# Filling products for the token assignment, another place for the compaction products, and a second bank for the row transpositions

## The chip, the cores and the metric

The kernel is one program on one core of a Trainium2 chip. Its metric is the device time of one execution in microseconds (us); the median of three runs of the kernel before is 1051.88 us (1051.66 to 1055.12). A core has TensorE (PE in the profile, PEld for its weight loads), VectorE (DVE), ScalarE (ACT), GpSimd (POOL) and SyncE (SP, which here only issues DMAs). TensorE's clock has two levels, 2.4 and 1.2 GHz; the profile gives the granted clock of a stretch as a share of the upper one, so 1.00 is full and 0.50 is half.

## What is computed

```python
x = attention(q, k, v, g_q, g_k)            # 4 x 12 heads x 448 rows x 64, with RMS norms
x = moe(x, modality_id, w_gate, bias, w1, w2)   # 1792 tokens, 8 experts, argmax
# second layer of experts: every expert takes CAP = 1792 / 8 = 224 tokens
logits = x @ w_gate
for idx in np.argsort(-logits.flatten()):
    tok, e = idx // 8, idx % 8
    if assigned[tok] >= 0 or counts[e] >= cap:
        continue
    assigned[tok] = e; counts[e] += 1
for e in range(8):
    mask = assigned == e
    h = np.maximum(x[mask] @ w1[e], 0.0)     # 768 x 1024
    out[mask] = h @ w2[e]                    # 1024 x 768
```

The greedy assignment of the second layer ("token assignment") is what the change touches, together with the start of that layer's experts.

## The kernel before, in words

The program runs attention, then the first layer of experts (`moe1`), then the second (`moe2`). The assignment is the class `Assigner`. It works in phases: in each phase every free token bids for its best open expert, the rank of each bid among all bids is counted, and one expert becomes full; its 224 tokens are then known and it can be computed. Phase 0 works on all 1792 tokens (16 columns of 128). After it the free tokens are compacted to 7 columns (in the branch that this input takes), and phases 1 to 6 and a last one work on those.

The steps of a phase, with their lines: `bids` takes the maxima on DVE and transposes the bids on PE (L1673), ACT copies the rows out (L1675). `count` compares every bid with every row on DVE or ACT and counts by products on PE (L1718, in phase 0 also L1618 and L1590 of `one` and `late`), and transposes the counts (L1792). `settle` finds who was served (L1819 to L1824 on DVE), sums that over the partitions on PE (L1827), and names the full expert. `put` writes one-hot rows (L1901 on DVE) and gathers the tokens' numbers by products on PE (L1906). `compact` calls the function `before` (a prefix sum with two products, L1926) and moves the free tokens together by 16 float32 products (L1997, two records each) of a one-hot matrix that DVE writes (L1995).

The experts: `gather` fetches the rows of an expert's tokens in two halves of 112 by an indirect DMA on POOL (L2124). `turn` transposes a quarter of them (three PE transpositions, L2132), and ACT copies them out (L2136); from the third expert on DVE also takes the lower part (L2139). Experts 0 and 1 run in float32 (first layer L2147, second L2184, two records for each product); experts 2 to 7 split weights and rows into two parts (L2114 on ACT, L2116 on DVE; first layer L2155 and L2156, second L2187 to L2189). Weights come by DMAs from SP (L2105). The four `turn`s of expert 0 write four banks of PSUM; those of all later experts write one bank, `px0`.

The order of the instructions on each engine is written by a planner, `Pace`. A step of the assignment is a Python `yield` of an engine (p, v, s, g for PE, DVE, ACT, POOL), a cost and the time from which it is ready. `work` says the same for a step of the experts; before it issues its own instruction it lets the assignment issue all steps that are ready up to that time (plus `SLACK` = 0.3 on PE). A later ready time thus puts an instruction further back in its engine's queue, behind work of the experts. All engines run their queues in order. The four turns of expert 0 have the ready times 4.5, 4.5, 5.5 and 5.5 in the planner's clock, and its first layer's first products are ready once the rows of turns 0 and 2 are copied.

PSUM has eight banks. In `moe2` banks 0 and 1 serve the assignment, `pg2` and `px0` the first-layer products, `po3` the second-layer results; the pool that holds them follows on the pools of `moe1`.

Of the kernel before, what the change touches and what calls it, by code (L numbers as in the profile page):

```python
# [10 lines left out]
F32 = mybir.dt.float32  # L11
# [9 lines left out]
CP, NC = 112, 4  # L21
# [766 lines left out]
def moe1(tc, consts, rt, e0, slot0, xs, wt, qkv, x0, w1, w2, w_gate2, y, assigner):  # L788
# [8 lines left out]
    with ExitStack() as ctx:  # L797
# [493 lines left out]
        t = turned(t)  # L1291
# [27 lines left out]

        pace.along(final())  # L1320
# [144 lines left out]
class Assigner:  # L1465
# [11 lines left out]
    def __init__(self, tc, consts, pool, bank, y, l2):  # L1477
        nc = tc.nc
        self.tc, self.c, self.bank = tc, consts, bank
# [57 lines left out]

    def fill(self, c, ti):

        nc, lo, x = self.tc.nc, self.lo, self.x3[:, c, :]  # L1540
        nc.vector.tensor_single_scalar(lo, ti, 127, op=OP.bitwise_and)
        nc.vector.tensor_copy(out=x[:, 0:1], in_=lo)
        nc.vector.tensor_tensor(out=x[:, 1:2], in0=ti, in1=lo, op=OP.subtract)
        nc.vector.tensor_scalar(self.busy[:, c : c + 1], ti, float(N), 100.0, op0=OP.is_ge, op1=OP.mult)
# [27 lines left out]
    def late(self):  # L1572

        nc, L = self.tc.nc, NTP - 1
        one, all_ = self.g[1:3]
        self.cols = NTP

        def earlier():
            yield "v", 1.1, 0.0
            self.below(L, one)  # L1580

        t, to = yield from self.bids(L, L + 1, 0.0, earlier)
        ct, t1 = yield from self.one(L, one, t, to, True)
        yield from self.all_scalar(L, all_, L - ON_S[1], L)
        yield from self.all_vector(NT, self.g14, ON_S[0], NT)
        t = yield from self.all_vector(L, all_, 0, L - ON_S[1])
        for n, g in (NT, self.g14), (L, all_):
            t = yield "p", 0.5, t
            for j in range(n):
                nc.tensor.matmul(ct[:, n, :], lhsT=g[:, 128 * j : 128 * j + 128], rhs=self.ohb[:, j, :E], start=False, stop=j == n - 1, skip_group_check=True)  # L1590
        t = yield "v", 0.2, t
        nc.vector.tensor_tensor(out=self.w, in0=self.w, in1=ct, op=OP.add)
        yield from self.settle(0, 0.0)
# [8 lines left out]
    def one(self, L, one, to, t, done):  # L1602
# [12 lines left out]
        t = yield "p", 0.5, max(t1, to)  # L1615
        for c in range(L, -1, -1):

            nc.tensor.matmul(ct[:, c, :], lhsT=one[:, 128 * c : 128 * c + 128], rhs=self.ohb[:, L, :E], start=c == L, stop=c < NT or not done, skip_group_check=True)  # L1618
# [35 lines left out]
    def bids(self, c0, c1, t, meanwhile=None):  # L1654
# [13 lines left out]
        for i in range(c0, min(c1, self.cols), 4):  # L1668
            v = min(4, c1 - i, self.cols - i)
            pr = self.bank().rearrange("p (a b) -> p a b", a=4)[:, :v]  # L1670
            tr[i] = yield "p", 0.11 * v, max(tb, tr.get(i - 8, 0.0))
            for a in range(v):
                nc.tensor.transpose(pr[:, a, :], self.bid[:, i + a : i + a + 1].to_broadcast([128, 128]), c["ident"])  # L1673
            tr[i] = yield "s", 0.2 + 0.1 * v, tr[i]
            nc.scalar.activation(self.rows[:, i : i + v, :], pr, AF.Copy)  # L1675
# [13 lines left out]
    def count(self, t, to, logits=None, more=None):  # L1689
# [100 lines left out]
        t = yield "p", 0.11 * G, t  # L1790
        for a in range(G):
# [16 lines left out]
    def settle(self, n, t):  # L1808
# [17 lines left out]
        tn = yield "p", 0.1, t  # L1826
# [55 lines left out]
    def put(self, n, t, ones, eng):  # L1882
# [21 lines left out]
        t = yield "p", 0.05 * C, t  # L1904
# [11 lines left out]
    def before(self, free, t):  # L1916
# [6 lines left out]
        t = yield "p", 0.12, t  # L1923
# [37 lines left out]
    def compact(self, F, t):  # L1961
# [30 lines left out]
        for j in range(C):  # L1992
# [3 lines left out]
            tp[j] = yield "p", 0.15, max(to, td)  # L1996
# [12 lines left out]
def moe2(tc, consts, qkv, x0, asn, w1, w2, y, out):  # L2009
# [10 lines left out]
    with ExitStack() as ctx:  # L2020
# [6 lines left out]
        asn.bank, asn.counts = lambda: next(turns), lambda: next(turns)  # L2027
# [37 lines left out]
        def phases(few):  # L2065
            t = 0.0
            for n in range(1, E - 1):

                to = (FEW if n == 1 else 0) if few else MANY.get(n)
                if to:  # L2070
                    t = yield from asn.compact(to, t)
# [54 lines left out]
        def turn(n, g, px=px0):  # L2126

            h, i = divmod(g, 2)
            px = px[:, : 3 * CP].rearrange("p (k c) -> p k c", c=CP)
            t = work("p", 0.3, ready[h])  # L2130
            for k in range(3):
# [201 lines left out]
NAT = 2  # L2333
GATHER = 1.7
# [71 lines left out]
```

## Time and profile before

| | |
|---|---|
| median of 3 runs | 1051.88 us |
| profiled execution | 1050.93 us, span 1049.2 us, mean granted clock 0.966 |
| PE busy | 993.0 us (95%), 6232 instructions |
| PEld busy | 777.7 us (74%) |
| DVE / ACT / POOL busy | 576.2 / 508.9 / 276.3 us |
| HBM | 110.69 MB read, 17.44 MB written |

A busy time counts an instruction from its start to its modelled end, and products overlap, so the distance from one start to the next is the price of a product in a stream. The span is divided roughly so: attention to about 400 us, the first layer of experts to about 683 us, the token assignment's phase 0 to 704 us, then the eight experts of the second layer to about 1037 us, and the last stores.

### The profile page before, as it was taken

Reading aid. Unit: us, or ns where it says so; the run is one execution under the profiler, and the core shown is the slowest. Engines: PE = TensorE matmul, PEld = TensorE weight load, DVE = VectorE, ACT = ScalarE, POOL = GpSimd, SP = SyncE. Lnnn points to the kernel's source line nnn. Section 1 sums busy time; section 2 is a strip of 40 time slices with the busy share of each in tenths; the row PEclk is TensorE's granted clock in tenths of the full one; section 3 lists DMA queues with packets and bytes.
Section 4 is the critical chain, followed back from the end, with each engine's and each line's share of the span. In section 5 each row is a group of like instructions: output and inputs, shape, how many; then the busy total and the mean of one; then the engine's idle time right before and its main releaser. Section 6 shows DMA issues by size and latency. Waiting matters only on the chain. (4 is left out here: it accounts for less than half of the span.)

```text
span 1049.2 us, 19190 instructions
## 1 busy us (share of the span) xinstructions
PE 993.0 (95%) x6232; PEld 777.7 (74%) x6232; DVE 576.2 (55%) x1543; ACT 508.9 (48%) x1127; POOL 276.3 (26%) x379
## 2 busy tenths in 40 slices
PE   8999999999998999999999998949999999999995
PEld 6666666666655688888888997738666789889995
DVE  5677877877875541111312121585878777666650
ACT  3777777777685422122441222641214466556640
POOL 5665555555522310100061111010010111011000
PEclk7799999999999999999999999967999999999998
DMA  7566666666365144628621011015932575585620
GB/s 160 124 148 155 145 150 159 145 151 162 86 183 188 32 173 147 219 93 290 229 71 33 32 62 37 17 48 231 327 113 91 190 243 174 201 278 149 217 78 29
DMA packets 80898, 151.05 MB, mean 144 GB/s; under 512 B 14254, under 2 KB 53422, under 8 KB 80752
## 3 DMA queue, kind: packets, MB, share of 16 engines
q1 hardware_dynamic: 75552, 126.06, 40.6%
q0 software_dynamic: 5200, 23.33, 7.2%
q8 instruction: 56, 0.92, 0.3%
q14 instruction: 90, 0.74, 0.2%
HBM read 110.69 MB, written 17.44 MB: 122 GB/s over the span
## 5 line engine op out<-in xcount | busy, mean ns | idle before, releaser
L224 DVE TENSOR_REDUCE nm<-sp 112x1 f32<-112x448 f32 x192 | 117.2, 620 | 69.3 <-PE sp L219 49.1
L230 ACT ACTIVATE e<-sp,nm 112x448 f32<-112x448 f32 x192 | 122.3, 638 | 29.4 <-DVE nm L224 25.5
L238 PE MATMUL tp<-ident,e 112*112 112x112 f32 x768 | 113.0, 271 | 0.0
L238 PEld LDWEIGHTS tp<-ident,e 112*112 112x112 f32 x768 | 82.5, 136 | 25.8 <-issue 16.4
L244 ACT ACTIVATE et<-tp 112x448 f32<-112x448 f32 x144 | 78.7, 546 | 39.6 <-PE tp L238 38.4
L2155 PE MATMUL bank<-xx,w1h 128*128 128x448 f32 x288 | 93.7, 381 | 0.0
L219 PE MATMUL sp<-bt,at 128*112 128x448 f32 x188 | 84.9, 452 | 1.0 <-DMA bt<-cut 0.4
L251 PE MATMUL op<-et,qkv 112*64 112x448 f32 x384 | 82.8, 552 | 0.0
L2195 POOL DMA_INDIRECT out_dram<-x,ids x16 | 17.0, 1064 | 247.4 <-ACT x L2194 157.5
L909 PE MATMUL pg<-w1h,xh 128*128 128x512 f32 x180 | 75.5, 419 | 6.5 <-PEq L1237 5.0
L932 PE MATMUL po<-w2h,hh 128*128 128x384 f32 x224 | 79.0, 353 | 0.1
L2156 PE MATMUL bank<-xx,w1l 128*128 128x224 f32 x288 | 77.2, 268 | 0.0
L933 PE MATMUL po<-w2l,hh 128*128 128x384 f32 x224 | 75.3, 336 | 0.1
L934 PE MATMUL po<-w2h,hl 128*128 128x384 f32 x224 | 75.3, 336 | 0.0
L911 PE MATMUL pg<-w1h,xl 128*128 128x512 f32 x180 | 71.6, 398 | 0.0
L910 PE MATMUL pg<-w1l,xh 128*128 128x512 f32 x180 | 71.5, 397 | 0.0
L2187 PE MATMUL bank<-w2h,hh 128*112 128x384 f32 x192 | 66.2, 345 | 0.0
L2189 PE MATMUL bank<-w2h,hl 128*112 128x384 f32 x192 | 64.6, 337 | 0.0
L2188 PE MATMUL bank<-w2l,hh 128*112 128x384 f32 x192 | 64.6, 337 | 0.0
L999 DVE COPY yt<-py 128x384 f32<-128x384 f32 x26 | 13.3, 552 | 90.6 <-PE py L998 90.6
L923 DVE TENSOR_TENSOR hl<-ph,hh 128x512 fp32r<-128x512 f32 x28 | 19.4, 691 | 79.4 <-ACT hh L922 47.4
L2116 DVE TENSOR_TENSOR w2l<-qkv,w2h 128x768 fp32r<-128x768 f32 x48 | 44.6, 957 | 26.9 <-ACT w2h L2114 20.8
(454 smaller groups left out, 2216.1 us busy)
## 6 DMA issues: line engine op xcount, KB each, us to landing
qkv<-in_moe_w_dram SPq DMA_DIRECT2D x88, 384.0 KB
qkv<-in_moe_w_dram SPq DMA_DIRECT2D x36, 512.0 KB
raw<-in_moe_w_dram SPq DMA_DIRECT2D x24, 512.0 KB
bt<-cut SPq DMA_DIRECT2D x96, 112.0 KB
at<-cut SPq DMA_DIRECT2D x96, 112.0 KB
w1s<-in_moe_w_dram SPq DMA_DIRECT2D x12, 512.0 KB
w2s<-in_moe_w_dram SPq DMA_DIRECT2D x16, 384.0 KB
qkv<-in_v_dram SPq DMA_DIRECT2D x12, 448.0 KB
```

What stands on the lines that cost most here:

```text
L219: nc.tensor.matmul(sp, lhsT=at[:, h, cs], rhs=bt[:, h, :], start=h == 0, stop=h == 1)
L224: nc.vector.tensor_reduce(out=st["nm"][:, n : n + 1], in_=sp, axis=AX.X, op=OP.max, negate=True)
L230: nc.scalar.activation(e, st.pop(("s", n)), AF.Exp, bias=st["nm"][:, n : n + 1], accum_out=st["sm"][:, n : n + 1])
L238: nc.tensor.transpose(tp[:, kc, :], e[:, kc * CP : (kc + 1) * CP], ident[:CP, :CP])
L244: nc.scalar.activation(dst, tp, AF.Copy)
L251: nc.tensor.matmul(st["op"][h * D : (h + 1) * D, :], lhsT=raws[i // 2][:, 2, 2 * (i % 2) + h, kc * D : (kc + 1) * D], rhs=st["et"][:, h, k ...
L909: nc.tensor.matmul(pg, lhsT=xh[:, k, :], rhs=w1h[:, k, fs], start=k == 0, stop=False)
L932: nc.tensor.matmul(po[n], lhsT=hh[:, k, :], rhs=w2h[:, kk, cs], start=kk == 0, stop=False)
L933: nc.tensor.matmul(po[n], lhsT=hh[:, k, :], rhs=w2l[:, kk, cs], start=False, stop=False)
L934: nc.tensor.matmul(po[n], lhsT=hl[:, k, :], rhs=w2h[:, kk, cs], start=False, stop=kk == KF - 1)
L2155: nc.tensor.matmul(pg, lhsT=h[:, k, fs], rhs=xx[:, k].rearrange("p a c -> p (a c)"), start=k == 0, stop=False)
L2156: nc.tensor.matmul(pg[:, :CAP], lhsT=l[:, k, fs], rhs=xh[:, k, :], start=False, stop=k == KD - 1)
```

## The change

A method `busy_pe(n)` issues n products of 512 columns of a matrix of ones into a bank that nothing reads (`spare`: a bank of `moe1` towards its end, `px0` at the start of `moe2`). It is called in front of ten kinds of PE steps of the assignment and once, with 16, in front of expert 0's first transposition; after that `spare` is `None` and no more are issued. The ready times of L1827 and L1906 in all phases but phase 0, and of L1926 where `spare` is `None`, become 0.4 later in the planner's clock; those of the compaction products (L1997) become 2.0 later. `turn` uses `px0` and `pg2[0]` in turn for all experts but the first.

```diff
--- before.py
+++ after.py
@@ -1317,6 +1317,7 @@
             yield "v", 0.1, t
             nc.vector.tensor_copy(out=asn.m[:, NTP - 1, :], in_=pl)
 
+        asn.spare = ps1.tile([128, 512], F32, name="pg")
         pace.along(final())
         pace.rest()
         send(yr, ti)
@@ -1476,7 +1477,7 @@
 
     def __init__(self, tc, consts, pool, bank, y, l2):
         nc = tc.nc
-        self.tc, self.c, self.bank = tc, consts, bank
+        self.tc, self.c, self.bank, self.spare = tc, consts, bank, None
         tile = lambda name, shape, dt=F32: pool.tile(shape, dt, name=name)
 
         self.m, self.l2 = l2[:, :, :E], l2
@@ -1535,6 +1536,14 @@
         self.mn, self.busyn, self.x3n = tile("mn", [128, most + 1, E]), tile("busyn", [128, most + 1]), tile("x3n", [128, most, 3])
         nc.gpsimd.memset(self.x3n, 1.0)
 
+    def busy_pe(self, n):
+
+        if self.spare is None:
+            return
+        ones = self.c["ones"]
+        for _ in range(n):
+            self.tc.nc.tensor.matmul(self.spare.rearrange("p (a b) -> p a b", a=4), lhsT=ones, rhs=ones.unsqueeze(1).to_broadcast([128, 4, 128]), start=True, stop=True)
+
     def fill(self, c, ti):
 
         nc, lo, x = self.tc.nc, self.lo, self.x3[:, c, :]
@@ -1586,6 +1595,7 @@
         t = yield from self.all_vector(L, all_, 0, L - ON_S[1])
         for n, g in (NT, self.g14), (L, all_):
             t = yield "p", 0.5, t
+            self.busy_pe(1 if n == NT else 4)
             for j in range(n):
                 nc.tensor.matmul(ct[:, n, :], lhsT=g[:, 128 * j : 128 * j + 128], rhs=self.ohb[:, j, :E], start=False, stop=j == n - 1, skip_group_check=True)
         t = yield "v", 0.2, t
@@ -1613,6 +1623,7 @@
         nc.vector.scalar_tensor_tensor(one[:, lo : lo + 128], flat[:, lo : lo + 128], self.bid[:, L : L + 1], self.tri, op0=OP.subtract, op1=OP.is_lt)
         ct = self.bank()[:, : (L + 1) * E].rearrange("p (c e) -> p c e", e=E)
         t = yield "p", 0.5, max(t1, to)
+        self.busy_pe(5 if done else 1)
         for c in range(L, -1, -1):
 
             nc.tensor.matmul(ct[:, c, :], lhsT=one[:, 128 * c : 128 * c + 128], rhs=self.ohb[:, L, :E], start=c == L, stop=c < NT or not done, skip_group_check=True)
@@ -1669,6 +1680,7 @@
             v = min(4, c1 - i, self.cols - i)
             pr = self.bank().rearrange("p (a b) -> p a b", a=4)[:, :v]
             tr[i] = yield "p", 0.11 * v, max(tb, tr.get(i - 8, 0.0))
+            self.busy_pe(6)
             for a in range(v):
                 nc.tensor.transpose(pr[:, a, :], self.bid[:, i + a : i + a + 1].to_broadcast([128, 128]), c["ident"])
             tr[i] = yield "s", 0.2 + 0.1 * v, tr[i]
@@ -1788,6 +1800,7 @@
         nc.scalar.activation(pcs[:r, x : 128 * G], pc[:r, x : 128 * G], AF.Copy)
         ct = self.bank().rearrange("p (a q w) -> p a q w", a=4, q=4)[:, :G]
         t = yield "p", 0.11 * G, t
+        self.busy_pe(3)
         for a in range(G):
             nc.tensor.transpose(ct[:, a].rearrange("p q w -> p (q w)"), pcs[:, 128 * a : 128 * a + 128], c["ident"])
         if more:
@@ -1823,7 +1836,8 @@
         with nc.allow_low_precision("counts up to 14"):
             nc.vector.tensor_reduce(out=self.ns, in_=u.rearrange("p c e -> p e c"), axis=AX.X, op=OP.add)
         pn = self.bank()[:, :E]
-        tn = yield "p", 0.1, t
+        tn = yield "p", 0.1, t + (LATER if n else 0.0)
+        self.busy_pe(6)
         nc.tensor.matmul(pn, lhsT=c["ones"], rhs=self.ns, start=True, stop=True)
 
         t = yield "v", unit, tu
@@ -1901,7 +1915,8 @@
             nc.vector.tensor_scalar(self.a[:, i, :], self.i112, k[:, i : i + 1], None, op0=OP.is_equal)
         t = max(t, tv)
         pi = self.bank()[:CP, : 4 * E]
-        t = yield "p", 0.05 * C, t
+        t = yield "p", 0.05 * C, t + (LATER if n else 0.0)
+        self.busy_pe(14)
         for j in range(C):
             nc.tensor.matmul(pi, lhsT=self.a[:, j, :], rhs=self.place[:, j, :], start=j == 0, stop=j == C - 1)
         table = self.table.rearrange("p e h w -> p e (h w)")
@@ -1920,7 +1935,8 @@
         f = self.fb[:, :P]
         t = yield "v", 0.1, t
         nc.vector.tensor_scalar(f, self.busy[:, :P], 50.0, None, op0=OP.is_lt)
-        t = yield "p", 0.12, t
+        t = yield "p", 0.12, t + (0.0 if self.spare else LATER)
+        self.busy_pe(8)
         pf = self.bank()[:, : 2 * P].rearrange("p (i c) -> p i c", i=2)
         for i, m in enumerate(("ut", "ones")):
             nc.tensor.matmul(pf[:, i, :], lhsT=c[m], rhs=f, start=True, stop=True)
@@ -1958,7 +1974,7 @@
         self.halves()
         yield from self.put(n, t, iter(range(self.cols)), nc.vector)
 
-    def compact(self, F, t):
+    def compact(self, n, F, t):
 
         nc = self.tc.nc
         C = self.cols
@@ -1993,7 +2009,7 @@
             o = self.g[j // have % 2].bitcast(F32)[:, 128 * (j % have) : 128 * (j % have) + 128]
             to = yield "v", 0.2, max(t, tp.get(j - 2 * have, 0.0))
             nc.vector.tensor_scalar(o, self.i128, b[:, j : j + 1], None, op0=OP.is_equal)
-            tp[j] = yield "p", 0.15, max(to, td)
+            tp[j] = yield "p", 0.15, max(to, td) + (BEHIND if n == 1 else LATER)
             nc.tensor.matmul(px, lhsT=o, rhs=data[:, j].rearrange("p n x -> p (n x)"), start=j == 0, stop=j == C - 1)
         px = px.rearrange("p (n x) -> p n x", n=F)
         t = yield "v", 0.5, tp[C - 1]
@@ -2024,7 +2040,7 @@
         bank = [ps.tile([128, 512], F32, name=f"bank{i}") for i in range(8)]
         pg2, po3, px0 = bank[2:4], bank[4:7], bank[7]
         turns = cycle(bank[:2])
-        asn.bank, asn.counts = lambda: next(turns), lambda: next(turns)
+        asn.bank, asn.counts, asn.spare = lambda: next(turns), lambda: next(turns), px0
 
         raws = [t[:, FF * i : FF * i + FF] for t in qkv for i in range(3)]
         xx = p2.tile([128, KD, 2, CAP], F32R, name="xx")
@@ -2068,7 +2084,7 @@
 
                 to = (FEW if n == 1 else 0) if few else MANY.get(n)
                 if to:
-                    t = yield from asn.compact(to, t)
+                    t = yield from asn.compact(n, to, t)
                 t = yield from asn.phase(n, t)
             yield from asn.last(E - 1, t)
 
@@ -2123,11 +2139,14 @@
             fetched.append((n, h))
             nc.gpsimd.indirect_dma_start(out=xgs[h], out_offset=None, in_=y, in_offset=IndirectOffsetOnAxis(ap=asn.ids[:, n, h : h + 1], axis=0))
 
-        def turn(n, g, px=px0):
+        def turn(n, g, px=None):
 
             h, i = divmod(g, 2)
-            px = px[:, : 3 * CP].rearrange("p (k c) -> p k c", c=CP)
+            px = (px or (px0, pg2[0])[g % 2])[:, : 3 * CP].rearrange("p (k c) -> p k c", c=CP)
             t = work("p", 0.3, ready[h])
+            if n == g == 0:
+                asn.busy_pe(16)
+                asn.spare = None
             for k in range(3):
                 nc.tensor.transpose(px[:, k, :], xgs[h][:, (3 * i + k) * 128 : (3 * i + k + 1) * 128], ident[:CP, :CP])
             yield
@@ -2331,6 +2350,8 @@
 EARLY = 0.3
 NHR = 5
 NAT = 2
+LATER = 0.4
+BEHIND = 2.0
 GATHER = 1.7
 FIRST = 1
 NHR = 5
```

## Rows read from the trace of the kernel before

**Rows 1.** Busy time by stretch: start:end, length, each engine's busy us, granted clock, DMA share, GB/s.
```profile
690.00:695.00 5.00, 2.12 (x46) 1.57 (x46) 4.63 (x11) 4.95 (x14) 0.00 (x0) 0.52 0.00 0
...
710.00:715.00 5.00, 5.00 (x28) 5.00 (x27) 2.04 (x13) 1.35 (x3) 0.00 (x0) 0.50 1.03 404
```

**Rows 2.** Timeline of PE, 705 to 722 us: start, us, line, out<-in, count, idle before.
```profile
708.20 0.82 PE L2132 MATMUL bank<-ident,xg 112*128 112x112 f32 x3 [3.71 <-DMA xg<-y,ids]
...
713.76 3.98 PE L1997 MATMUL bank<-rows,g 128*128 128x77 f32 x18
717.54 1.78 PE L2147 MATMUL bank<-xtt,w1s 128*128 128x224 f32 x4
...
721.17 2.44 PE L2147 MATMUL bank<-xtt,w1s 128*128 128x224 f32 x12
```

**Rows 3.** Timeline of PE, 656 to 661 us, after a pause.
```profile
656.56 0.80 PE L909 MATMUL pg<-w1h,xh 128*128 128x512 f32 x1 [4.98 <-PEq L1237]
...
658.01 0.63 PE L909 MATMUL pg<-w1h,xh 128*128 128x512 f32 x1
658.43 0.63 PE L910 MATMUL pg<-w1l,xh 128*128 128x512 f32 x1
...
660.10 0.39 PE L909 MATMUL pg<-w1h,xh 128*128 128x512 f32 x1
660.33 0.39 PE L910 MATMUL pg<-w1l,xh 128*128 128x512 f32 x1
```

**Rows 4.** Timeline of PE, 691 to 705 us: steps of phase 0 that wait.
```profile
691.58 0.47 PE L1673 MATMUL bank<-ident,bid 128*128 128x128 f32 x1 [1.05 <-DVE w L1805]
...
700.64 1.90 PE L1906 MATMUL bank<-place,g 128*112 128x32 bf16 x16 [3.32 <-POOL place L1893]
704.29 0.17 PE L1926 MATMUL bank<-fb,ut 128*128 128x16 bf16 x1 [1.75 <-DVE fb L1922]
```

**Rows 5.** Timeline of all engines, 692 to 706 us: work beside those steps.
```profile
692.46 0.35 DVE L1613 SCALAR_TENSOR_TENSOR g<-rows,bid,tri 128x128 bf16<-128x128 f32 x1 [0.27 <-ACT rows L1675]
692.73 2.35 DVE L1628 TENSOR_TENSOR g<-rows,bid 128x512 bf16<-128x512 f32 x2
...
699.26 2.95 DVE L1901 TENSOR_SCALAR g<-i,k 128x112 bf16<-128x112 bf16 x13
...
705.52 0.94 POOL L2124 DMA_INDIRECT xg<-y,ids  x1 [0.30 <-DVE t L1934]
```

**Rows 6.** DMA issues, 706 to 707.5 us: count, median us from issue to landing.
```profile
xg<-y,ids POOLq DMA_INDIRECT x1, 6.0
```

**Rows 7.** Chain that ended last, 744 to 860 us: start, us, what.
```profile
744.99 0.83 PE bank L2184 x2
...
747.09 0.29 PE bank L2132 x3
...
855.00 5.36 DMA qkv<-in_moe_w_dram
```

**Rows 8.** Timeline of PE, 843 to 848 us: around two transpositions of expert 2.
```profile
843.69 0.33 PE L2189 MATMUL bank<-w2h,hl 128*112 128x384 f32 x1
844.58 0.51 PE L2132 MATMUL bank<-ident,xg 112*128 112x112 f32 x3 [0.56 <-DVE xx L2139]
...
846.84 0.33 PE L2189 MATMUL bank<-w2h,hl 128*112 128x384 f32 x1
847.27 0.51 PE L2132 MATMUL bank<-ident,xg 112*128 112x112 f32 x3
```

**Rows 9.** Timeline of PE, 800 to 1000 us: products that stood idle before their start.
```profile
803.62 0.51 PE L2132 MATMUL bank<-ident,xg 112*128 112x112 f32 x3 [0.53 <-DVE xx L2139]
...
862.52 0.17 PE L1827 MATMUL bank<-ns,ones 128*128 128x8 bf16 x1 [0.69 <-DVE ns L1824]
...
935.54 0.22 PE L1906 MATMUL bank<-place,g 128*112 128x32 bf16 x1 [2.29 <-DVE g L1901]
...
989.22 0.51 PE L2132 MATMUL bank<-ident,xg 112*128 112x112 f32 x3 [0.57 <-DVE xx L2139]
```

## The prediction

> **What bounds the kernel now.** I read the granted clock by stretch first, then PE's timeline where it is low, then the chain that ended last, then the products that stood idle. Four things are to be seen.
>
> From 690 to 720 us the clock is at half. Between 690 and 695 PE is busy for 2.12 of 5.00 us; between 710 and 715 it is busy all the time and still has 0.50 [rows 1]. That second stretch holds row transpositions and compaction products L1997, and these do not bring the clock back: 18 records of L1997 take 3.78 us, 0.21 each [rows 2]. Only expert 0's first layer brings it back: its first four records stand about 0.39 apart, those from 721.17 on 0.20 [rows 2].
>
> Up to 708.20 the assignment itself is the bound, a chain of short steps on DVE, ACT and PE, and PE stands idle in it: 1.05 us before L1673, 3.32 before L1906, 1.75 before L1926, 3.71 before the first row transposition [rows 2, 4].
>
> From 708.20 to the layers' end PE is the bound, with work in its queue all the time.
>
> From expert 2 on PE halts at two kinds of places: at row transpositions, which wait until DVE has read the one bank of the group before, and at assignment steps at an expert's start, which wait for DVE [rows 8, 9].
>
> **The fillers.** The trace of before has no bfloat16 product of 512 columns over the whole array. The nearest rows are L909 and L910, 512 columns: 0.42 us apart at half clock, 0.23 at full [rows 3]. I take 0.23 where the clock holds and keep 0.42 for the range; less than nothing is excluded for the product itself, because its result is not read and its gain is the clock. In phase 0's tail there are 3 in front of L1792, 1 and 5 in front of L1618, 6 of L1673, 1 and 4 of L1590, 6 of L1827, 14 of L1906, 8 of L1926, 16 of the first row transposition.
>
> At full clock 14 take 3.2 us of 3.32 idle, 8 take 1.84 of 1.75, 16 take 3.7 of 3.71 [rows 2, 4]: covered to a tenth each. L1906 has more cover: its 16 products follow the one-hots of L1901, which DVE writes for 2.95 us from 699.26 on [rows 5]. If that cover is gone (fillers at half clock) each overruns, which is a rival below.
>
> The six in front of L1673 are the exception. L1673 waited for DVE's L1805, the last reader of the earlier pool's banks [rows 4], though its own input, the bids, needs no such step. The fillers write a bank of the same new pool. If they wait for the same release, they start at 691.58 and L1673 is 6 x 0.23 = 1.4 late; if their bank is free they start when PE ran dry, 691.58 - 1.05 = 690.53, and end at 691.9, 0.35 late. I take 1.2, near the first, because the row shows a release by a reader of the old pool. Queued behind L1673 is ACT's copy L1675, and for that waits L1613 on DVE [rows 5]; L1628 follows it in DVE's queue, L1590 waits for L1628, and the rest of phase 0 hangs on that. So 1.2 us are lost on the path, up to the gathers and weight issues.
>
> **Expert 0's layer ahead of the compaction.** By the ready times, L1997 (about 4.8 in the planner's clock, now 2.0 more) no longer stands between the four turns (4.5 and 5.5). The first layer is ready when turns 0 and 2 are copied, 7.6 by my working of the planner's costs (four transposition groups of 0.3 up to 6.1, then copies of 0.45). By then six of the sixteen compaction products (12 records) are ready and go ahead of it, and ten (20 records) go among its first products. PE thus waits for the second half of the rows: issued at 705.52, 6.0 to landing [rows 5, 6], 711.5, and with the 1.2 from above 712.7. Two transposition groups at full clock, 0.29 each [rows 7], and 12 records at 0.105 (half of 0.21) end at 714.5. That is the start of L2147, in place of 717.54 [rows 2].
>
> From that start to L2184 before were 744.99 - 717.54 = 27.45 us [rows 2, 7], of which the 3.63 us up to 721.17 ran at half clock: at full 1.8 less. With 20 records of L1997 (2.1) among them, L2184 starts at 714.5 + 25.65 + 2.1 = 742.25. Gain 2.7 us, the 1.2 already off. The compaction ends some microseconds later against the layer; its customer, expert 1's tokens, has over 20 us of slack, since expert 1 begins only when expert 0's second layer is done.
>
> **Two banks.** At an expert's second group the last product starts at 843.69 and the next could go 0.175 later, but the transposition starts at 844.58: 0.71 lost; at the third 847.27 - 846.84 - 0.175 = 0.26 [rows 8]; the fourth I take as the third. That is 1.2 us for each of experts 2 to 6, and 0.5 for expert 1, where only the second group waits [rows 9]. With two banks a group waits for the reader of the group before the last, which is done by then. It counts only where PE bounds: in experts 1, 5 and 6 (of six such waits, one in each expert, rows 9 show the first and the last). In experts 2 to 4 PE waits anyway at the next expert's first assignment step (three waits, 0.69 the first and 2.29 the last [rows 9]) for DVE, which waits for weights whose DMA took 5.36 us [rows 7]; there the saved time turns into a longer wait. Sum 0.5 + 2 x 1.2 = 2.9. A new wait is possible: the next layer's first product writes `pg2[0]`, which the fourth group now holds until it is copied; it is copied ten microseconds before.
>
> **The later ready times.** 0.4 in the planner's clock lets one or two pairs of first-layer products (0.32 each in the code) go ahead of L1827, L1926 or L1906. At the three waits at expert starts that is 0.3 to 0.6 each: I take 1.2 in all. It is no loss unless a step moves to a place where DVE is later still: bounds 0 and 3.7 (all three waits gone) and, for a shifted step, one more wait of 2.3 to the bad.
>
> **Sum.** 2.7 + 2.9 + 1.2 = 6.8 us. The profiled execution took 1050.93 (span 1049.2 and 1.73 around it), 0.95 below the median of 1051.88; it gives 1044.1, and the median 1045.1.
>
> **Rivals.** *The clock falls again before the first layer.* Between the last filler and L2147 lie two transposition groups, an idle wait of 2 to 3 us for the second half of the rows, two more groups and 12 compaction records. For it: the dense stretch of the same instructions at 0.50 [rows 1], and the half clock after a pause of 4.98 us [rows 3]. Against: this stretch is shorter than the 30 us at half clock of before. The Trainium skill ("TensorE: Matmul & The Clock Gate", Part 4: PE-mode transpose) says that transposes do not count as PE activity in the way products do; the trace agrees, with 0.50 in a stretch with PE fully busy. Time: two groups at 0.56 (708.20 to the next start) and 12 records at 0.21 put L2147 at 716.35, 3.6 us at half lose 1.8, and L2184 starts at 716.35 + 25.65 + 2.1 + 1.8 = 745.9, 0.9 late. With 2.9 and 1.2: gain 3.2, 1048.7.
>
> *The banks bring nothing.* DVE and the weights bound all experts from 2 on. Against: in experts 5 and 6 no assignment step waits at the start. Then 2.7 + 0.5 + 0.6 = 3.8: 1048.1.
>
> *Slower: the fillers are the new wait.* If the clock has fallen by 691 us and the fillers do not bring it back, each costs 0.42: six 2.5 late, 14 take 5.9 of 3.32 (2.6 late), 8 take 3.4 of 1.75 (1.6), 16 take 6.7 of 3.71 (3.0): 9.7 late in place of 1.2, so 8.5 worse than my sum, 1053.6, and with the first layer at half clock 1056. It decides from the point where fillers before L1906 still run at half. Against: dense 512-column products brought the clock back between 656.56 and 660.10 [rows 3], and at half clock the fillers are dense.
>
> **Chances.** My forecast 0.48, the falling clock 0.25, no gain from the banks 0.15, fillers as the wait 0.08; 0.04 for steps of the assignment that land badly. About 0.5% (5.3 us, the time 1046.6) is what a measurement of this kernel can tell. The forecast's own range is 1041.5 to 1047.5, so most of it and a fifth of the second case are faster: 0.50; same 0.42; slower 0.08. Eight in ten lie between 1041 and 1050.
>
> **What would show it.** Right: granted clock near 1.00 from 695 on; fillers 0.2 apart; L2147 starting near 714 at 0.2 apart; no PE idle before L2132 from expert 1 on. Wrong: fillers 0.42 apart in front of L1906; a first row transposition after 710; the first records of L2147 at 0.39; longer waits before L1827 or L1906 by what the banks saved.

## The result and the profile after

| | before | after |
|---|---|---|
| median of 6 runs | 1055.73 us (1051.66 to 1057.85) | 1041.05 us (1037.0 to 1053.93) |
| profiled execution | 1050.93, span 1049.2 | 1044.16, span 1042.4 |
| mean granted clock | 0.966 | 0.974 |
| PE busy | 993.0 (x6232) | 1000.5 (x6296) |
| DVE / ACT busy | 576.2 / 508.9 | 575.6 / 505.8 |

The ratio of after to before is 0.9888 (0.9852 to 0.9924), some 11.8 us of the forecast's 1051.88. The six runs of before include the three of the forecast; the slowest run of after, 1053.93, fell in a slower state and is left out of the ratio. The two profiled executions are 6.8 us apart, but the part of the program that no edit touches took 3.1 us longer in the profile of after. So all marks below are counted from a fixed point, the last product with the router's weights (L1033): 685.20 us before, 688.28 after. Over the fourteen profiles of this case that point lies between 682.3 and 691.3, with no edit ahead of it; the runs do not show why it varies. Counted from it, the experts' last product ends at 351.3 before and at 341.7 after: 9.7 us.

The stretches of low clock, after (start:end, length, busy us of PE, PEld, DVE, ACT, POOL, then the granted clock, DMA share, GB/s):

```profile
692.00:693.00 1.00, 1.00 (x5) 0.54 (x3) 1.00 (x2) 1.00 (x5) 0.00 (x0) 0.50 0.00 0
...
695.00:700.00 5.00, 4.47 (x47) 2.34 (x46) 3.60 (x9) 3.45 (x7) 0.00 (x0) 1.00 0.00 0
...
705.00:710.00 5.00, 4.39 (x26) 2.50 (x25) 3.61 (x20) 0.28 (x1) 1.39 (x2) 0.86 0.33 107
710.00:715.00 5.00, 5.00 (x24) 2.26 (x23) 3.71 (x14) 0.00 (x0) 1.12 (x3) 0.80 0.74 187
715.00:720.00 5.00, 4.23 (x38) 4.02 (x35) 3.10 (x18) 1.58 (x4) 0.00 (x0) 1.00 1.03 378
```

The clock still falls twice, near 692 and near 709, for some 3 us each, and not for 30 us as before [rows 1]. Where expert 0's layer begins it is full. PE's timeline there (L1545 are the fillers; L2151, L2013 and L2166 are the row transpositions, compaction products and first layer that were L2132, L1997 and L2147):

```profile
691.47 1.42 PE L1545 MATMUL pg<-ones 128*128 128x512 bf16 x3
...
695.52 1.46 PE L1545 MATMUL bank<-ones 128*128 128x512 bf16 x6 [0.96 <-DVE w L1818]
696.81 0.27 PE L1685 MATMUL bank<-ident,bid 128*128 128x128 f32 x1
...
702.10 3.18 PE L1545 MATMUL bank<-ones 128*128 128x512 bf16 x14
705.57 1.86 PE L1921 MATMUL bank<-place,g 128*112 128x32 bf16 x16 [0.28 <-POOL place L1907]
707.75 2.76 PE L1545 MATMUL bank<-ones 128*128 128x512 bf16 x8 [0.32 <-issue]
...
710.41 4.41 PE L1545 MATMUL bank<-ones 128*128 128x512 bf16 x16
714.65 0.74 PE L2151 MATMUL bank<-ident,xg 112*128 112x112 f32 x6
716.16 0.79 PE L2151 MATMUL bank<-ident,xg 112*128 112x112 f32 x6 [0.77 <-DMA xg<-y,ids]
716.79 1.47 PE L2013 MATMUL bank<-rows,g 128*128 128x77 f32 x12
718.10 0.59 PE L2166 MATMUL bank<-xtt,w1s 128*128 128x224 f32 x2
```

The six fillers before L1685 (L1673 before) wait for the same reader of the old pool as that instruction did [rows 4], start with its release at 695.52 and put it 1.29 us back. The 14 before L1921 fit: they take 3.18 us, and L1921 then still waits 0.28 for POOL. The 8 ran partly at half clock (2.76 us for the group) and held the prefix sum back: it starts at 710.31, 22.0 from the mark, 19.1 before. But the first layer of expert 0 starts when the second half of its rows has come (716.16) and 12 compaction records are through, at 718.10: 29.8 from the mark, 32.3 before [rows 2], with products 0.2 apart.

Who PE waited for from expert 0's layer to the end, after (us in total, times, longest); below it the waits of before at the starts of experts 3 to 5:

```profile
PE bank L2174 <- DVE hr L2182: 2.9, 4, 1.3
PE bank L1730 <- DVE g L1765: 1.1, 1, 1.1
PE bank L1921 <- DVE g L1915: 0.9, 2, 0.5
PE bank L2151 <- DMA xg<-y,ids: 0.2, 1, 0.2
```

```profile
PE bank L1906 <- DVE g L1901: 2.3, 1, 2.3
PE bank L1926 <- DVE fb L1922: 0.7, 1, 0.7
PE bank L1827 <- DVE ns L1824: 0.7, 1, 0.7
```

No transposition waits for DVE any more, and the three waits of before at an expert's start are gone, the one of 2.29 us among them [rows 9]. Other steps of the assignment wait in their place, for 2.0 us in all (L1730 and L1921), and PE waits in the first layers of experts 3 to 6 (L2174) for DVE's part of the relu, which frees its banks.

### The profile page after: what moved, and what is told of

Read it like the earlier page. It is cut to its first block, busy times and chain, and to the rows that moved or that the text cites. A ratio compares the mean times of both kernels' runs of the same rounds, so it can differ in the third digit from the quotient of the medians.

```text
span 1042.4 us, 19307 instructions
## 1 busy us (share of the span) xinstructions
PE 1000.5 (96%) x6296; PEld 779.8 (75%) x6296; DVE 575.6 (55%) x1543; ACT 505.8 (49%) x1127; POOL 275.2 (26%) x379
## 5 line engine op out<-in xcount | busy, mean ns | idle before, releaser
L238 PEld LDWEIGHTS tp<-ident,e 112*112 112x112 f32 x768 | 82.9, 137 | 25.9 <-issue 16.3
L2174 PE MATMUL bank<-xx,w1h 128*128 128x448 f32 x288 | 93.2, 379 | 2.9 <-DVE hr L2182 2.9
L2174 PEld LDWEIGHTS bank<-xx,w1h 128*128 128x128 f32 x288 | 54.1, 188 | 9.5 <-DVE hr L2182 4.0
```

Of the source, the lines that this page charges most:

```text
L238: nc.tensor.transpose(tp[:, kc, :], e[:, kc * CP : (kc + 1) * CP], ident[:CP, :CP])
L2174: nc.tensor.matmul(pg, lhsT=h[:, k, fs], rhs=xx[:, k].rearrange("p a c -> p (a c)"), start=k == 0, stop=False)
```

## The experiments

Each kernel was profiled once and timed beside the kernel before. The marks are in us from the last L1033, read from PE's timelines: the first row transposition of expert 0 (T), the start of its first and of its second layer, the start of the second layers of experts 2 and 5, and the end of the last expert. "Ratio" is of time to that of before, with its interval.

| kernel | T | first layer 0 | second layer 0 | second layer 2 | second layer 5 | end | ratio |
|---|---|---|---|---|---|---|---|
| before | 23.0 | 32.3 | 59.7 | 155.2 | 265.4 | 351.3 | |
| after | 26.4 | 29.8 | 55.7 | 149.4 | 257.5 | 341.7 | 0.9888 (0.9852 to 0.9924) |
| after, again | 25.8 | 29.7 | 55.6 | 149.0 | 256.5 | 340.5 | 0.9897 (0.9856 to 0.9937) |
| no fillers | 22.9 | 29.9 | 58.6 | 152.0 | 259.4 | 342.8 | 0.991 (0.988 to 0.9941) |
| one bank | 25.7 | 29.5 | 55.4 | 148.8 | 255.9 | 342.0 | 0.9902 (0.9865 to 0.9939) |
| 16 fillers alone | 25.0 | 28.8 | 54.6 | 148.0 | 255.3 | 339.1 | 0.9855 (0.9825 to 0.9886) |
| LATER = 0 | 25.7 | 29.3 | 55.8 | 149.8 | 257.7 | 341.8 | 0.9898 (0.9864 to 0.9932) |
| BEHIND = 0 | 25.8 | 31.5 | 56.3 | 148.8 | 254.8 | 338.0 | 0.9875 (0.9836 to 0.9914) |
| only the banks | 22.8 | 32.3 | 59.7 | 154.4 | 272.6 | 356.6 | 1.0035 (1.0008 to 1.0062) |
| only the fillers | 26.4 | 31.7 | 57.4 | 152.9 | 264.7 | 350.7 | 0.9989 (0.9953 to 1.0025) |
| only LATER | 23.1 | 32.6 | 59.8 | 152.3 | 259.0 | 345.0 | 0.9926 (0.9893 to 0.996) |
| LATER and banks | 23.1 | 32.3 | 58.8 | 151.3 | 259.8 | 343.1 | 0.9907 (0.9874 to 0.9939) |
| 16 fillers, BEHIND = 0 | 25.0 | 29.7 | 54.5 | 147.0 | 254.4 | 338.7 | 0.9832 (0.9792 to 0.9872) |
| the same, LATER = 0.8 | 24.4 | 29.6 | 54.0 | 146.3 | 250.6 | 335.4 | 0.9822 (0.9778 to 0.9865) |

The intervals of the times overlap for most of these; the marks separate them better, since they leave out the part ahead. Two profiles of the changed kernel differ by 1.2 us at the end, so an end that differs by less says nothing.

**The changed kernel again.** No edit.

> The changed kernel itself, beside the other three on one chip. All marks are counted from the last product with the router's weights (L1033, 685.20 us in the profile of before, 688.28 in that of after), because the part ahead of it differs by 3.1 us between those two profiles without any edit there. Theory: the change is worth what lies behind that mark, 9.7 us in the two profiles (last product of the experts at 351.3 before, 341.7 after): time 0.987 to 0.993 of before; first layer of expert 0 starts near 30, its second layer near 56. Rival: the mark itself moves by an effect of the change, then the stretch ahead of it is longer than before's again by about 3 us.

The gain is behind the mark again, 10.8 us, and the marks are as in the first profile. The theory holds. The rival's longer stretch ahead came (691.3), but kernels with some of the edits have their mark anywhere from 682.3 to 690.0, so the runs do not tie it to the change.

**Without fillers.**

```diff
     def busy_pe(self, n):
-        if self.spare is None:
-            return
+        return
```

> The changed kernel without any filling product. Theory (the fillers' gain is the clock at expert 0's first layer): the clock is at half from about 5 us after the mark (the last router product) on; nothing delays the gathers, so the second half of the rows lands at 26.3, two transposition groups (0.56 each) and 12 compaction records (0.21 each) follow, the first layer starts at 30.0 and runs at half for about 3 us or more; its second layer starts at 58 to 59 (55.7 with fillers, 59.7 in the kernel before), and the kernel is 2 to 3 us slower than the changed one. Rival (the order alone does it: the layer comes before the compaction and wakes the clock itself early): second layer at 55.5 to 56.5, time within 1 us of the changed kernel.

Busy time by stretch and PE's timeline without fillers:

```profile
710.00:715.00 5.00, 3.12 (x16) 3.12 (x16) 2.51 (x15) 1.35 (x3) 0.00 (x0) 0.50 1.02 402
715.00:720.00 5.00, 5.00 (x21) 4.85 (x21) 0.00 (x0) 0.00 (x0) 0.00 (x0) 0.50 1.02 410
720.00:725.00 5.00, 5.00 (x30) 4.82 (x30) 2.15 (x12) 0.91 (x2) 0.00 (x0) 0.85 0.85 341
```

```profile
713.06 2.71 PE L2012 MATMUL bank<-rows,g 128*128 128x77 f32 x12
715.56 1.04 PE L2165 MATMUL bank<-xtt,w1s 128*128 128x224 f32 x2
...
721.56 0.59 PE L2165 MATMUL bank<-xtt,w1s 128*128 128x224 f32 x2
```

The first layer starts at 29.9, as early as with fillers, because it waits for the rows in both; but it runs at half clock until about 721, and the second layer starts at 58.6: 3.0 late, as the theory said. At the end 1.1 and 2.3 us are left of it, against the two profiles of the changed kernel.

**One bank.**

```diff
-            px = (px or (px0, pg2[0])[g % 2])[:, : 3 * CP]...
+            px = (px or px0)[:, : 3 * CP]...
```

> The changed kernel with the row transpositions of experts 1 to 7 in the one bank of before. Theory: the waits for the reader of the one bank come back in all of experts 1 to 6; they cost 0.5 to 1.1 us at expert 1 and about 1.3 each at experts 5 and 6, while in experts 2 to 4 the loss is regained at the next wait for DVE: 3 to 4 us slower than the changed kernel, with the experts' end at 345 to 346 after the mark. Rival (DVE and the weights bound every expert from 2 on): end within 1 us of the changed kernel's 341.7.

PE's waits with one bank, same columns as above:

```profile
PE bank L2151 <- DVE xx L2158: 3.0, 5, 0.7
PE bank L1921 <- DVE g L1915: 0.2, 1, 0.2
```

The waits for the one bank's reader come back in five experts (not in expert 1), and the waits of the first layers for DVE go. Up to the second layer of expert 5 one bank is 0.6 to 1.6 ahead of the two profiles with two banks, at the end 0.3 and 1.5 behind. So the theory's size (3 to 4) is not there, and the rival's end (within 1 us of 341.7) is; a table below shows where the gain went.

**Only the 16 fillers ahead of the first transposition.** All the other calls of `busy_pe` get 0, as these two:

```diff
-            self.busy_pe(1 if n == NT else 4)
+            self.busy_pe(0)
...
-        self.busy_pe(14)
+        self.busy_pe(0)
```

> The changed kernel with only the 16 fillers ahead of the first row transposition, none in front of the assignment's own steps. Theory (the fillers ahead of L1673 and L1805 delay the gathers by 1.8 us, and only the last ones are needed for the clock): the gathers' second half lands at 26.3 after the mark, the 16 fillers start at 19.3 at half clock and bring the clock up within 3 to 4 us, the first layer starts at 28.2 (29.8 in the changed kernel) with products 0.2 apart, second layer at 54: 1 to 2 us faster than the changed kernel. Rival (the clock needs the earlier fillers as well): the 16 run at half for 6.9 us, the first layer starts at 30 at half clock, second layer at 57 or later: 1 to 2 us slower.

PE's timeline with the 16 alone:

```profile
702.14 5.73 PE L1545 MATMUL bank<-ones 128*128 128x512 bf16 x16
707.71 0.74 PE L2151 MATMUL bank<-ident,xg 112*128 112x112 f32 x6
709.48 0.80 PE L2151 MATMUL bank<-ident,xg 112*128 112x112 f32 x6 [1.04 <-DMA xg<-y,ids]
...
711.43 0.59 PE L2166 MATMUL bank<-xtt,w1s 128*128 128x224 f32 x2
```

Theory right in kind: the 16 start at half clock, end before the second half of the rows has come, and the layer runs at 0.2 from its first product. It starts 1.0 us earlier than with all fillers, and the end comes 1.4 to 2.6 us earlier. So the other 48 cost 1 us at expert 0 and give nothing back.

**LATER = 0, then BEHIND = 0,** each in the changed kernel.

```diff
-LATER = 0.4
+LATER = 0.0
```

> The changed kernel with LATER = 0 (L1841, L1921 and L1942, the sums, token tables and prefix sums after phase 0, ready as early as before). All marks from the last router product. What is open: without any filler the changed order still brings 8.5 of 9.7 us (342.8 against 351.3), and with one bank 342.0; so most of the gain is neither. Theory A (the later ready times remove PE's waits at the starts of experts 3 to 5): the waits of 0.7, 0.7 and 2.3 us in front of those three steps come back, the experts' end goes from 340.5 to 343 to 345. Theory B (the shift of the compaction by 2.0 moves all later steps of the assignment, and with them the places where they wait): the end stays within 1 us of 340.5 and no wait of 2 us stands before an assignment step.

```diff
-BEHIND = 2.0
+BEHIND = 0.0
```

> The changed kernel with BEHIND = 0 (the compaction products stand between the transpositions of expert 0's rows as before). Theory A: the first layer starts where the compaction ends; DVE's one-hots end about 29.8 after the mark, so the layer starts at 30.5 to 31.5 (29.7 in the changed kernel), its second layer at 56.0 to 57.0, and behind that nothing changes: end at 341 to 342.5. Theory B (the order at expert 0 also sets where the later assignment steps wait): one of the waits of 0.7 to 2.3 us at the starts of experts 3 to 5 comes back, end at 343 to 345.

Without LATER the end, 341.8, moves by 0.1 to 1.3 us, and no wait in front of an assignment step is longer than 1.1 us: theory A's waits do not come back, and theory B misses its bound of 1 us by 0.3 at most. Without BEHIND the layer starts at 31.5 and its second layer at 56.3, as theory A put it, but the end is 2.5 to 3.7 earlier, which neither theory had. So BEHIND buys 0.7 us at expert 0's second layer and costs more behind it, and neither of the two is needed while the other is there. The next two runs have neither, and also lack the fillers or the second bank.

**Only the banks.**

```diff
     def busy_pe(self, n):
...
+        return
...
-LATER = 0.4
-BEHIND = 2.0
+LATER = 0.0
+BEHIND = 0.0
```

> The kernel before with the two banks alone: no fillers, LATER = 0 and BEHIND = 0. Theory (a bank counts only where PE bounds): the first layer starts at 32.3 and the second at 59.7 as before; experts 5 and 6 gain 0.8 to 1.3 us each, experts 2 to 4 nothing: end at 348.5 to 350 (before 351.3). Rival (the banks bring the most): end at 345 or less.

Missed by both: the two banks by themselves make the kernel 5.3 us slower at the marks and slower in time. PE's waits, then the chain that ended last around the first of them:

```profile
PE bank L1840 <- DVE ns L1836: 4.4, 2, 4.2
PE bank L1941 <- DVE fb L1936: 3.7, 1, 3.7
PE bank L1920 <- DVE g L1914: 3.5, 1, 3.5
```

```profile
850.34 8.88 DMA qkv<-in_moe_w_dram
859.32 0.85 ACT w2h L2129
860.20 0.96 DVE w2l L2131
861.16 0.19 DVE ns L1836
861.55 0.31 PE bank L2173
```

At the start of expert 3 PE's queue has the assignment's L1840 at its head; that needs a sum (L1836) which stands in DVE's queue behind the split of a late piece of the weights, and behind L1840 stand first-layer products that are ready. While PE waits its clock falls, and these products then run at half. Busy time by stretch around the second of the waits, at expert 4:

```profile
895.00:898.00 3.00, 1.78 (x12) 1.53 (x11) 0.00 (x0) 0.00 (x0) 0.00 (x0) 1.00 1.02 296
898.00:900.00 2.00, 0.00 (x0) 0.00 (x0) 0.64 (x1) 1.52 (x3) 0.00 (x0) 0.84 1.01 402
900.00:902.00 2.00, 1.55 (x7) 1.46 (x7) 1.86 (x5) 1.45 (x4) 0.00 (x0) 0.50 1.02 404
902.00:904.00 2.00, 2.00 (x8) 1.82 (x8) 0.00 (x0) 0.00 (x0) 0.96 (x1) 0.50 1.06 377
```

The first wait is the wait of 0.69 in [rows 9], now 4.2, because PE arrives 1.4 earlier and the weights 2.1 later (counted from the start of expert 2's second layer, that piece lands at 22.1 and at 19.9 before; its DMA took 8.88 us and 5.36 [rows 7]). Why the DMA took longer was not tried.

**Only the fillers.**

```diff
-            px = (px or (px0, pg2[0])[g % 2])[:, : 3 * CP]...
+            px = (px or px0)[:, : 3 * CP]...
...
-LATER = 0.4
-BEHIND = 2.0
+LATER = 0.0
+BEHIND = 0.0
```

> The kernel before with the fillers alone: one bank, LATER = 0 and BEHIND = 0. Theory: the first row transposition at 25.7 (23.0 before), the compaction products at full clock but ahead of the layer, which starts at 30.5 to 31.5 and runs 0.2 apart; second layer at 56.5 to 57.5 (59.7 before); behind it the waits of before return at the same places: end at 347.5 to 349. Rival (a shift of the whole assignment against the experts, by whatever cause, removes the waits): end at 344 or less.

The layer begins at 31.7 and the second layer at 57.4, about as put; the end, 350.7, is 1.7 us later than the theory's latest, and the rival is further off. So 2.3 us are won at expert 0 and lost in the first layers of experts 3 and 4, 0.9 and 3.4 longer than before (expert 5's gives 2.7 back). At expert 4 a wait in front of an assignment step, which before was 0.7 there, has grown, and the clock is below full from 896 to 902 behind it:

```profile
895.70 0.17 PE L1942 MATMUL bank<-fb,ut 128*128 128x8 bf16 x1 [2.54 <-DVE fb L1937]
```

**Only the later ready times,** then **with the banks.** LATER alone:

```diff
     def busy_pe(self, n):
...
+        return
...
-            px = (px or (px0, pg2[0])[g % 2])[:, : 3 * CP]...
+            px = (px or px0)[:, : 3 * CP]...
...
-BEHIND = 2.0
+BEHIND = 0.0
```

> The kernel before with the later ready times alone (LATER = 0.4): no fillers, one bank, BEHIND = 0. Marks from the last router product. Theory (the 0.4 moves the assignment's products off the places where they stand behind DVE's weight split, and works without the rest): first layer at 32.3 and second layer at 59.7 as before, experts' end at 344 to 347 (before 351.3), no wait above 1.2 us in front of an assignment step. Rival (it works only with the shift of the compaction or with the banks): end at 349 or more.

With the banks the middle edit is left out:

```diff
     def busy_pe(self, n):
...
+        return
...
-BEHIND = 2.0
+BEHIND = 0.0
```

> The later ready times and the two banks, no fillers, BEHIND = 0. The banks alone ended at 356.6, 5.3 us later than before, with waits of 4.2, 3.7 and 3.6 us in front of assignment steps. Theory (the banks pay only once those steps have left that place): end at 340 to 342, about 15 us below the banks alone and 2 to 4 below the later ready times alone. Rival (it was the compaction's shift that turned the banks' loss): end at 348 or more.

LATER alone takes 6.3 us off, as the theory put it; it is the most of the three edits that were tried alone. All its waits are those of the one bank:

```profile
PE bank L2150 <- DVE xx L2157: 3.0, 5, 0.7
```

None is left in front of an assignment step. What moved can be counted in PE's timelines: between the second layers of experts 2 and 3 there is 1 record of the assignment before and 23 with LATER; in experts 0 and 1 there are 260 before and 240 with it, the difference being 20 of the 168 counting products L1718. So 0.4 is no local delay: whole steps change their place, out of experts 0 and 1 (2.9 of the 6.3 us are won up to expert 2's second layer) and away from the starts of experts 4 and 5. The code shows how it can add up, since several steps of a phase that follow one another get the 0.4; no run gives it to one of them alone.

The largest piece, 4.0 us, is expert 5's first layer. Before, the wait of 2.29 in [rows 9] stands in it, and the clock falls behind that wait. Busy time by stretch, before, then two stretches of the same layer with LATER:

```profile
934.00:936.00 2.00, 0.46 (x3) 0.44 (x4) 1.60 (x4) 1.55 (x4) 0.00 (x0) 1.00 1.04 412
936.00:938.00 2.00, 2.00 (x9) 1.87 (x8) 1.74 (x5) 0.97 (x3) 0.75 (x1) 0.50 1.01 401
938.00:940.00 2.00, 2.00 (x9) 1.84 (x9) 0.39 (x1) 0.39 (x2) 0.37 (x1) 0.65 1.00 387
940.00:942.00 2.00, 2.00 (x14) 1.89 (x13) 0.74 (x2) 0.72 (x2) 0.00 (x0) 1.00 0.93 369
```

```profile
936.00:938.00 2.00, 2.00 (x15) 1.90 (x14) 1.75 (x7) 1.02 (x3) 0.00 (x0) 1.00 1.02 400
938.00:940.00 2.00, 2.00 (x15) 1.88 (x14) 1.72 (x5) 1.62 (x5) 0.21 (x1) 1.00 1.03 408
```

A wait of 2.29 us thus cost 4.0: 9 records in 2 us follow it in place of 14, until the clock is back. With LATER PE is full there, at 1.00 throughout.

With the banks on top of LATER the end is 343.1; these two edits are worth 8.2 together where the banks alone lose 5.3. The theory (the banks pay only once the assignment's steps have left that place) holds in kind, while its numbers are missed narrowly: the end is 343.1 and not 340 to 342, 13.5 us below the banks alone and not 15, 1.9 below LATER alone and not 2 to 4.

The runs so far can be read as steps of one edit each, from before to the changed kernel: LATER 6.3 us (351.3 to 345.0), the banks 1.9 (to 343.1), BEHIND 0.3 (to 342.8, the kernel without fillers), the fillers 1.1 to 2.3 (to 341.7 and 340.5). These shares hold for this order only. Taken out of the changed kernel one at a time, LATER is worth 0.1 to 1.3, the banks 0.3 to 1.5, the fillers 1.1 to 2.3, and BEHIND costs 2.5 to 3.7; that does not add up to the 9.7. BEHIND alone was not run, nor the fillers and the banks with both constants at 0.

**Where the banks' gain goes.** The time from the start of one part to the next, in us, from the same timelines (the second layer of an expert contains the transpositions for the next expert, the first layer the waits for DVE and the weights):

| kernel | second layers 2, 3, 4, 5 | first layers 3, 4, 5, 6 |
|---|---|---|
| before | 19.35, 19.47, 19.34, 19.32 | 16.14, 16.20, 19.63, 15.19 |
| only the banks | 17.96, 18.39, 17.97, 17.96 | 21.23, 21.75, 20.86, 15.98 |
| only LATER | 19.71, 19.42, 19.58, 19.35 | 16.83, 15.59, 15.60, 15.18 |
| after | 18.36, 17.95, 18.13, 17.96 | 18.92, 17.08, 17.70, 16.14 |
| one bank | 19.72, 19.43, 19.58, 19.34 | 16.84, 15.62, 15.92, 15.37 |
| the best (below) | 17.97, 18.45, 17.97, 18.02 | 17.33, 16.84, 15.74, 15.59 |

Two banks take some 1.4 us off every second layer, in all kernels. In the first layers of the table it is lost again: between one bank and after, 5.7 us are saved in the four second layers and 6.1 lost in the four first layers, where PE, ahead of time, halts for DVE. At expert 5 the loss is 0.8 of 1.4, and at expert 6, which the table leaves out, nothing is lost: its second layer takes 17.97 in place of 19.34, and the first layer behind it 15.18 in both. Alone, the banks bring PE to the assignment steps so early that the clock falls too, at three experts.

**The best version.** The 16 fillers alone, with one more edit and then with two:

```diff
-        self.busy_pe(14)
+        self.busy_pe(0)
...
-BEHIND = 2.0
+BEHIND = 0.0
```

> The changed kernel with the 16 fillers ahead of the first row transposition alone, and BEHIND = 0: the two edits that each gave a shorter run (ends 339.1 and 337.6). Theory (they add, since one is worth 1 us ahead of expert 0's layer and the other 2 to 3 us behind it): transposition at 25.0, first layer at 30.4, second at 55.2, end at 336 to 337.5, time 0.982 to 0.987 of before. Rival (the gain of BEHIND = 0 was chance of where DVE's waits fell): end at 339 to 341.

```diff
-        self.busy_pe(14)
+        self.busy_pe(0)
...
-LATER = 0.4
-BEHIND = 2.0
+LATER = 0.8
+BEHIND = 0.0
```

> The same with LATER = 0.8 in place of 0.4. Theory (a longer delay lets more of the experts' products go ahead of a waiting assignment step): the remaining waits of 0.4 to 1.1 us in front of such steps shrink below 0.3, end 0.5 to 1.5 us earlier than with 0.4. Rival (PE now waits there for the experts' own relu on DVE and for the weights, whatever stands in its queue): end within 1 us of it.

The 16 fillers with BEHIND = 0 end at 338.7, between the theory's 337.5 and the rival's 339: against the 16 alone BEHIND = 0 brings 0.4 us there, less than two profiles of one kernel differ, so the two edits do not add. (The 337.6 in the text on record is 338.0 from the mark of the table.) With LATER = 0.8 the end is 335.4, 3.3 us earlier, more than either theory put: one wait for the relu is left, at expert 3,

```profile
855.36 0.47 PE L2174 MATMUL bank<-xx,w1h 128*128 128x448 f32 x1 [1.17 <-DVE hr L2182]
```

```profile
PE bank L2174 <- DVE hr L2182: 1.2, 1, 1.2
PE bank L2151 <- DMA xg<-y,ids: 0.9, 1, 0.9
```

but none in front of an assignment step, and the first layers of experts 5 and 6 are short. Its median, 1033.43 us, is the lowest of all kernels here, 0.9822 of before; against the changed kernel's 0.9888 the intervals overlap, and the marks put it 5 to 6 us ahead.

## Why the prediction was right, and where its terms were off

The direction was right, and the median, 1041.05 us, lies at the very edge of the range given eight in ten (1041 to 1050), just under the forecast's own 1041.5 to 1047.5. The gain was put too small: 6.8 us, where the ratio gives some 11.8 and the marks 9.7 and 10.8. That the two profiled executions differ by just the 6.8 us that were put is luck, since the profile of after lost 3.1 us in the untouched part.

*Expert 0's layer: 2.7 put, 4.0 measured.* The working held: transposition groups, the DMA's second half as the bound, 12 records ahead and 20 among the first products. The second half was put at 27.5 from the mark and came at 27.9, the layer's start at 29.3 and 29.8. The delay by the six fillers was put at 1.2 and is 1.3. What was put too long is the rest of the layer: 27.75 from its start to the second layer, measured 25.9. The layer at full clock had its right size, for with only the fillers it takes 25.7 where 25.65 was put; but the compaction's records, put at 2.1, make it only 0.2 longer. Some 1.2 us of the difference are 20 of the assignment's counting products (L1718) that no longer stand in the layer, 32 in place of 52; the rest is open.

One sign of being wrong came: the first row transposition starts at 714.65, 26.4 from the mark, where 710 would be 24.8. It cost nothing, because the layer waits for the second half of the rows, which comes later still.

*Fillers.* Put as free of cost but for the six: so it is for the layer's start, though 3, 1 and 8 of them ran at half clock and delayed steps. The rival of the clock that falls again before the layer did not come; it fell earlier, while fillers were running, and came back. What the fillers are worth is 1.1 to 2.3 us at the end with the rest of the change, and 0.7 without it, less than two profiles of one kernel differ.

The Trainium skill says that transposes do not count as PE activity in the way products do ("TensorE: Matmul & The Clock Gate", Part 4: PE-mode transpose). The run without fillers does not speak against it, with 0.50 from 710 to 715 us, but PE is also idle there for 1.9 of 5.00 us, and in [rows 1] compaction products stand beside the transpositions; so no run here shows the transposes by themselves.

*Two banks: 2.9 put, 0.3 to 1.5 measured* (one bank against two in the changed kernel). The price per expert was about right: 1.2 put, 1.4 measured. That the saved time turns into a longer wait in experts 2 to 4 was right too, but so does 0.8 of expert 5's, behind other waits than the three of [rows 9]; expert 6's stays. The 0.5 at expert 1 is not there: one bank reaches the second layer of expert 2 at 148.8, two at 149.0 and 149.4. In the changed kernel this comes near the rival by which the banks bring nothing; alone they lose 5.3, which no rival had.

*Later ready times: 1.2 put, 6.3 measured alone, 0.1 to 1.3 when taken out of the changed kernel.* This is the step whose mechanism failed. The prediction had "0.4 in the planner's clock lets one or two pairs of first-layer products (0.32 each in the code) go ahead", and so 0.3 to 0.6 at each of three waits. It read the constant as a local delay; the runs show whole steps in other places, 23 records in place of 1 between the second layers of experts 2 and 3, and no wait left in front of an assignment step. The bound that was named, 3.7, was too small twice: it counted the waits without the half clock behind the longest (1.7 us), and not what is won up to expert 2's second layer (2.9). That 1.2 fits what the term is worth in the changed kernel is luck. There BEHIND also shifts the assignment; whether it does the same work was not tried, as BEHIND alone was not run.

*The sum.* It took the terms as independent. They are not: LATER is worth 6.3 us alone and 0.1 to 1.3 beside the rest, and the banks cost 5.3 us alone and bring 1.9 on top of LATER.

*The slower rival* had its mechanism in the profile (8 fillers at half clock, the prefix sum late) without its price, because the gathers need the tokens' table (L1921) and not that sum: the first goes out at 709.12, ahead of it.

## What to carry over

When a list scheduler writes the queues, a small constant in it is not a local delay: count, per stage, the instructions that change place, and look whether they leave a stage where the engine is full for one where it waits. A transposition that no longer waits only pays if nothing behind it in the queue waits for a slower engine; measure such an edit with its companions and alone. To raise TensorE's clock for a dense layer it was enough here to fill the last wait ahead of it; and a wait of some microseconds in the midst of dense work is priced with the slow products behind it, not by its own length.

## What was not expected of the hardware

Dense 77-column float32 products with their weight loads and row transpositions kept PE busy for 5.00 of 5.00 us at a granted clock of 0.50 [rows 1], and after 16 fillers of 512 columns (5.73 us) it was full. In the midst of a dense first layer a wait of 2.29 us was followed by some 3.5 us at half clock. The same weight piece of 384 KB took 5.36 us by DMA in one kernel and 8.88 in another, with the same number of transfers issued meanwhile. And the part ahead of the mark, the same in all kernels, took 682.3 to 691.3 us in the fourteen profiles, 3.1 apart in the two of the changed kernel.
